# A spectral filter and a routed expert layer: the weights' maxima spread by TensorE, five experts loaded through SyncE, rank products moved

## The chip, the cores and the metric

The program runs on one core of a Trainium2 chip. Its engines are TensorE (PE, with its weight load PEld), VectorE (DVE), ScalarE (ACT), GpSimd (POOL) and SyncE (SP, which issues DMA transfers). The metric is the device time of one execution in microseconds, as the median of the runs shown; lower is better. Profiles are of one execution each.

## The reference

```
X = rfft(x, axis=1); y = irfft(X * (filt_r + 1j * filt_i), n=2496)      # x: 8 x 2496 x 256
x = y.reshape(19968, 256)
xn = x / (norm(x) + 1e-6); en = expert_emb / (norm(expert_emb) + 1e-6)  # 8 experts
logits = xn @ en.T / tau; expert_idx = argmax(logits)
probs = exp(logits - max); probs /= sum + 1e-9; gate = probs[expert_idx]
for e in range(8):                                                      # w1: 256 x 1024, w2: 1024 x 256
    out[mask] = gate * (relu(x[mask] @ w1[e]) @ w2[e])
```

Everything is fp32 at the outside. Each token goes to one expert.

## The kernel before

The 8 batches are 8 groups. A length of 2496 is 64 x 39, so the transform is a product over 39, one over 64, the filter, and the two inverse products. For a batch g these are `conv_s1` (tiles s), `conv_s2` (tiles s2, then the filter in yy and xs, then sa) and `conv_sb` (tiles y: the inverse over 39). The first batch has its own form, `conv_first`: its first product and its turned copies stay in SBUF, inside the array W in which the experts' weights will lie later (`turned`, `filter_first`). yy and xs are made by VectorE and added by POOL (L527, L621 for later batches).

`conv_sb` also routes. Of 8 token tiles (a chunk) `route` makes logits, the one-hot tile oh and, by products on TensorE (rk, "rank products", L812 to L815), each token's place in its expert's list. Then POOL scatters each row to DRAM (XS, L841), one scatter for a tile; `rows_out` casts the place to an integer on VectorE ahead of each (L834). A route is a generator with three steps; `part` takes one step of it and sends out one tile's scatter, twice in an iteration of `conv_sb`.

Then come slots. A slot is 256 rows of one expert: its rows come transposed from XS (xT), `up` makes ph and h (h in two f16 parts, ScalarE and VectorE), `down` makes po, and the output is scattered by POOL (L941). A slot has four steps fp. Group 0 has 8 slots, one an expert, and runs beside the stages of batch 1; so on for each group, and at last come blocks of 128 rows for what didn't fit.

An expert's weights are used as two f16 parts, high and low, scaled by a power of two. For that `weight_load` fetches w1 and w2 as fp32 (1 MB each) into the place of the next expert in W; `weight_halves` searches the largest magnitude: `largest` on VectorE within a partition (L258), `spread_max` over the partitions, which is an all-reduce on POOL (L262). Then `scales` makes the factors and `halves` the parts: ScalarE the high part (L284, L285, L289), POOL (L286) or VectorE (L290) the low one. `weight_halves` is a generator (`prep`): for each expert the search of the next one, then four quarters of its halves. The eighth expert's weights come last, in two parts.

What sets the order: while the first batch runs (`head`), the four engines but POOL keep the order of the program text (`manual_schedule`), and two tables of step numbers say at which steps a weight load (`WLOADS`) and a step of `prep` (`PREPS`) stand. After it a scheduler orders all engines by its own timeline; `spread`, called twice in each fp, takes a step of `prep`, and of the loads at each second call. A slot can't begin before its expert's halves are written (`prepped`). POOL is ordered by the scheduler throughout. Each engine runs its instructions strictly in its order.

Of the kernel before, what the change touches and what calls it, by code (L numbers as in the profile page):

```python
# [51 lines left out]
FAHEAD = 6  # L52
WLOADS = (4, 7, 11, 15, 21, 27)
PREPS = (15, 17, 23, 25, 27, 29, 31, 33, 41, 45, 49, 53, 57, 61)


@with_exitstack
def moe_spectral_kernel(
# [117 lines left out]
    def experts_ready():  # L176
# [10 lines left out]
        ehl = cw.tile([E, 2, D], F16, tag="hl", bufs=XYB, name="ehl")  # L187
        nc.scalar.copy(ehl[:, 0], esc)
        nc.vector.tensor_tensor(out=ehl[:, 1], in0=esc, in1=ehl[:, 0], op=ALU.subtract)
# [18 lines left out]
    wmax = const.tile([P, E, 2], F32, tag="wmax", name="wmax")  # L208
    wall = const.tile([P, E, 2], F32, tag="wall", name="wall")
    wsc = const.tile([P, E, 2], F32, tag="wsc", name="wsc")  # L210
# [30 lines left out]
    def weight_loads():  # L241

        for e in range(E - 1):
            for j in range(2):
                weight_load(nc.scalar, e, j)
                yield
# [3 lines left out]
    def weight_halves():  # L250
# [10 lines left out]
        def spread_max(e, js):  # L261
            nc.gpsimd.partition_all_reduce(wall[:, e, js], wmax[:, e, js], P, bass.bass_isa.ReduceOp.max)  # L262

        def scales(e, js):
            v.tensor_scalar(out=wall[:, e, js], in0=wall[:, e, js], scalar1=2.0 ** -100, scalar2=None, op0=ALU.max)
            v.tensor_scalar(out=wsc[:, e, js].bitcast(I32), in0=wall[:, e, js].bitcast(I32), scalar1=0x7F800000,
                            scalar2=0x7F800000, op0=ALU.bitwise_and, op1=ALU.bitwise_xor)
            for j in range(js.start, js.stop):
                v.tensor_scalar(out=wsc[:, e, j:j + 1], in0=wsc[:, e, j:j + 1], scalar1=2.0 ** (13 if j else 5),
                                scalar2=None, op0=ALU.mult)  # L270
            v.reciprocal(winv[:, e, js], wsc[:, e, js])
            if js.stop == 2:
                v.tensor_tensor(out=isc[:, e:e + 1], in0=winv[:, e, 0:1], in1=winv[:, e, 1:2], op=ALU.mult)
# [18 lines left out]
        def maxima(e):  # L292
            while (e, 1) not in raws:
                next(loads)
            for j in range(2):
                largest(e, j)
                if j:
                    spread_max(e, slice(0, 2))
                yield
# [12 lines left out]
        for j, order in ((0, (0, 1)), (1, (3, 2))):  # L312
            yield
            weight_load(nc.sync, e, j)
            yield
            yield
            largest(e, j)
            spread_max(e, slice(j, j + 1))
            yield
            scales(e, slice(j, j + 1))  # L320
            for k in order:
                halves(e, k)
                yield
# [133 lines left out]
    HALF = P * NK2  # L457
    turned = [big[:, n * 2 * HALF:(n + 1) * 2 * HALF].rearrange("p (h q) -> p h q", h=2) for n in range(2)]
    by_k2 = [t.rearrange("p h (q k) -> p h q k", k=NK2) for t in turned]

    def filter_first(k2):

        at = 4 * HALF + k2 * CW
        if at + CW <= big.shape[1]:
            ft = big[:, at:at + CW].rearrange("p (r c) -> p r c", r=2)
# [296 lines left out]
    def route(g, out_rows, t0, n, rows, ssq, rr, lp):  # L762
# [42 lines left out]
        yield 1  # L805

        base = state["base"]
        state["base"] = nbase = rt.tile([P, E], F32, tag="base", name=f"base{tg}")
# [284 lines left out]
    with tc.manual_schedule(engines=engines):  # L1093
        for n, _ in enumerate(head()):
            if n in WLOADS:
                next(loads, None)
            if n in PREPS:
                next(prep, None)
# [11 lines left out]
    def spread():  # L1110

        run["n"] = run.get("n", -1) + 1
        if run["n"] % 2 == 0:
            next(loads, None)
# [129 lines left out]
```

## Time and profile before

| what | value |
|---|---|
| median of 3 runs | 1433.49 us (1433.06 to 1438.99) |
| profiled execution, its own time | 1423.8 us |
| its span | 1422.0 us, mean granted clock of TensorE 0.94 |
| TensorE busy | 1260.9 us (89%) |
| VectorE, ScalarE, POOL busy | 872.5 (61%), 707.6 (50%), 562.9 us (40%) |
| DMA | 218.68 MB, mean 154 GB/s |

Busy time counts instructions that compute; an engine that waits or issues a transfer isn't busy. A row of waits names who waited, for which work, the sum, how often and the longest. In a timeline the bracket at the end of a row is the idle time before it and what ended it ("issue": nothing that the profile shows). The granted clock is a share of 2.4 GHz, so 0.50 is 1.2 GHz.

### The profile page before, as it was taken

The page shows a single profiled execution, that of the slowest core. Times are in us where ns is not written, and L with a number is a line of the kernel's source. Part 1 is how long each engine was busy: PE and PEld are TensorE (multiplying, and loading weights), DVE is VectorE, ACT ScalarE, POOL GpSimd, SP SyncE. Part 2 cuts the span into 40 slices and gives each one's busy share as a digit, 9 for nine tenths or more (in the row PEclk, how much of TensorE's full clock was granted, in tenths as well). Part 3 has the DMA queues.
Part 4 walks back from the last instruction along what each step waited for, and adds up shares of the span by engine and source line. Part 5 has one row for each costly group of instructions (what it writes and reads, how often), then busy time and mean ns, then how long its engine had stood idle before and what let it go on. Part 6 is the DMA issues. An engine that isn't in the chain of part 4 may idle for free.

```text
span 1422.0 us, 32280 instructions
## 1 busy us (share of the span) xinstructions
PE 1260.9 (89%) x11144; PEld 1000.3 (70%) x11144; DVE 872.5 (61%) x2842; ACT 707.6 (50%) x1600; POOL 562.9 (40%) x630
## 2 busy tenths in 40 slices
PE   6546275889699989999999999999999999999998
PEld 5333153557376876778687778777787888999997
DVE  2637457748447675867567576658567832366664
ACT  3456045646256465557646664755576333333333
POOL 1323412524542753464264527444631741222221
PEclk8868578899799999999999999999999999999999
DMA  8312395465777777676767666766764432122221
GB/s 292 125 45 79 94 307 187 149 163 158 210 205 191 194 222 188 167 210 196 207 161 217 200 173 186 225 193 165 200 185 120 112 95 52 43 53 50 47 44 42
DMA packets 221610, 218.68 MB, mean 154 GB/s; under 512 B 125197, under 2 KB 166125, under 8 KB 219520
## 3 DMA queue, kind: packets, MB, share of 16 engines
q1 hardware_dynamic: 192558, 141.44, 38.3%
q0 software_dynamic: 26592, 60.28, 13.7%
q10 hardware_dynamic: 2290, 14.81, 2.8%
q8 instruction: 93, 1.52, 0.5%
q14 instruction: 77, 0.63, 0.1%
HBM read 116.37 MB, written 79.60 MB: 138 GB/s over the span
## 4 chain that ended last, share of the span: by engine, by line
PE 41%; issue 11%; DMA 5%; POOL 4%; DVE 2%; ACT 2%; SPq 0%; POOLq 0%; DVEq 0%; ACTq 0%
PE ph L1006 15%; PE po L1034 14%; PE y L427 4%; POOL out_dram L941 3%; PE s L427 2%; PE sa L432 2%; PE s L432 2%; PE tp L736 2%; DMA a<-SD 1%; DMA f<-ZD 1%; DMA ZD<-z 1%; PE lp L751 1%; DMA XS<-rows,ixi 1%; DMA f<-in_filt 1%; DVE xs L587 1%
## 5 line engine op out<-in xcount | busy, mean ns | idle before, releaser
L1034 PE MATMUL po<-W,h 128*128 128x256 f16 (+1 forms) x3864 | 499.8, 274 | 1.2 <-ACT h L1012 1.0
L1006 PE MATMUL ph<-xT,W 128*128 128x256 f16 x3072 | 405.2, 277 | 47.3 <-DMA xT<-XS 24.5
L1034 PEld LDWEIGHTS <-h 128*128 128x128 f16 x3864 | 370.7, 98 | 88.0 <-issue 44.5
L1006 PEld LDWEIGHTS <-W 128*128 128x128 f16 x3072 | 298.6, 99 | 136.5 <-issue 92.0
L1012 ACT ACTIVATE h<-ph 128x512 f16<-128x512 f32 (+1 forms) x388 | 203.8, 526 | 302.1 <-PE ph L1006 233.6
L1013 DVE SCALAR_TENSOR_TENSOR h<-ph,h 128x512 f16<-128x512 f32 (+1 forms) x388 | 231.9, 598 | 189.5 <-ACT h L1012 187.7
L941 POOL DMA_INDIRECT out_dram<-o,meta x161 | 171.7, 1066 | 316.8 <-ACT o L1041 270.2
L841 POOL DMA_INDIRECT XS<-rows,ixi x176 | 174.6, 992 | 124.6 <-issue 71.7
L621 POOL TENSOR_TENSOR yy<-yy,xs 128x512 f32<-128x512 f32 x70 | 93.6, 1343 | 99.0 <-DVE xs L587 66.7
L387 POOL DMA_DIRECT2D in<-in_x x84 | 67.7, 807 | 145.4 <-PE s L427 114.7
L1006 PE MATMUL ph<-xT,wp 128*128 128x128 f16 x1584 | 104.8, 219 | 0.0
L1006 PEld LDWEIGHTS <-wp 128*128 128x128 f16 x1584 | 96.7, 98 | 2.6
L994 DVE COPY wp<-W 128x1024 f16 x132 | 61.3, 465 | 49.6 <-PE ph L1006 48.9
L717 ACT ACTIVATE rows<-y 128x256 f16<-128x256 f32 x176 | 66.2, 385 | 48.5 <-PE y L427 47.9
L692 DVE SCALAR_TENSOR_TENSOR rows<-y,rr,rows 128x256 f16<-128x256 f32 x176 | 77.1, 478 | 20.1 <-ACT rows L689 18.4
L427 PE MATMUL s<-in,c_sb 117*128 117x512 f32 (+1 forms) x168 | 87.7, 608 | 1.4 <-ACT z L642 1.2
L427 PE MATMUL y<-f,csb_sb 120*128 120x512 f32 (+1 forms) x168 | 83.1, 579 | 4.1 <-DMA f<-ZD 4.0
L689 ACT ACTIVATE rows<-y,rr 128x256 f16<-128x256 f32 x176 | 74.0, 475 | 24.9 <-DVE rr L722 23.3
L585 DVE TENSOR_TENSOR yy<-s,f 128x256 f32<-128x256 f32 x140 | 53.1, 419 | 51.1 <-ACT xs L614 45.0
L1041 ACT ACTIVATE o<-po,meta 128x256 f32<-128x256 f32 x161 | 69.5, 475 | 24.1 <-PE po L1034 23.3
L451 ACT COPY s<-s 128x512 f32<-128x512 f32 x77 | 45.3, 588 | 53.8 <-PE s L427 49.5
L587 DVE SCALAR_TENSOR_TENSOR xs<-xs,sgn_sb,f 128x256 f32<-128x256 f32 x140 | 68.6, 531 | 0.0
(196 smaller groups left out, 1502.3 us busy)
## 6 DMA issues: line engine op xcount, KB each, us to landing
f<-in_filt SPq DMA_DIRECT2D x148, 256.0 KB
a<-SD SPq DMA_DIRECT2D x70, 256.0 KB
ZD<-z SPq DMA_DIRECT2D x70, 256.0 KB
SD<-s SPq DMA_DIRECT2D x70, 240.0 KB
f<-ZD SPq DMA_DIRECT2D x70, 240.0 KB
in<-in_x POOLq DMA_DIRECT2D x70, 234.0 KB, 4.4
W<-in_w ACTq DMA_DIRECT2D x14, 1024.0 KB
W<-in_filt SPq DMA_DIRECT2D x12, 256.0 KB
```

The source lines that it names most:

```text
L427: nc.tensor.matmul(out_, c[:a.shape[0]], a, start=True, stop=True)
L587: nc.vector.scalar_tensor_tensor(out=o, in0=i, scalar=sgn_sb[:, k2:k2 + 1], in1=f, op0=ALU.mult, op1=ALU.mult)
L621: nc.gpsimd.tensor_tensor(out=yy, in0=yy, in1=xs, op=ALU.add)
L689: nc.scalar.activation(rows[:, i, 0:D], y[:, i], AF.Copy, scale=rr[:, u:u + 1])
L692: nc.vector.scalar_tensor_tensor(out=rows[:, i, D:2 * D], in0=y[:, i], scalar=rr[:, u:u + 1], in1=rows[:, i, 0:D], op0=ALU.mult, op1=ALU.s ...
L841: i = nc.gpsimd.indirect_dma_start(out=XS, out_offset=bass.IndirectOffsetOnAxis(ap=ix, axis=0), in_=src, in_offset=None)
L941: i = nc.gpsimd.indirect_dma_start(out=out, out_offset=bass.IndirectOffsetOnAxis(ap=idx, axis=0), in_=o, in_offset=None, bounds_check=NT - ...
L1006: last["pe"] = nc.tensor.matmul(ph[:, fi, :size], wp[:, k * 2 + wh, fi * P:(fi + 1) * P], xT[:, xh * 2 + k], start=(c == 0), stop=(c == 5))
L1012: last["relu"] = nc.scalar.activation(h[:, 0, :, :size], ph[:, :, :size], AF.Relu)
L1013: hd = nc.vector.scalar_tensor_tensor(out=h[:, 1, :, :size], in0=ph[:, :, :size], scalar=0.0, in1=h[:, 0, :, :size], op0=ALU.max, op1=ALU. ...
L1034: nc.tensor.matmul(self.po[:, s], self.hs[fp][:, hh, fi, s * P:(s + 1) * P], self.Wp[:, off + wh * 1024:off + wh * 1024 + D], start=(fp == ...
L1041: nc.scalar.activation(o, self.po[:, s], AF.Copy, scale=self.meta[:, s, 1:2])
```

## The change

Four things change. `spread_max` no longer uses POOL: the maxima are cut to a power of two, a product of TensorE with a unit matrix turns a column of 128 maxima into a row (pm), VectorE takes the row's maximum (wtop) and writes it on a small diagonal (wdg), and a second product with ones spreads it to all partitions (ps). These are two further steps of `prep` for each search. The loads of the head go through SyncE in place of ScalarE, and ten stand there in place of six, five experts; to make room `turned[1]` moves to the end of W. `PREPS` has 24 steps in place of 14, the last eight at the head's last step: four experts are searched and two split there, before three and two. And in the first batch the first two chunks' rank products wait three steps of `part` longer.

```diff
--- before.py
+++ after.py
@@ -50,8 +50,8 @@
 DLAG = 2
 MID = 8
 FAHEAD = 6
-WLOADS = (4, 7, 11, 15, 21, 27)
-PREPS = (15, 17, 23, 25, 27, 29, 31, 33, 41, 45, 49, 53, 57, 61)
+WLOADS = (0, 1, 8, 12, 30, 34, 38, 42, 46, 50)
+PREPS = (16, 20, 22, 24, 26, 30, 36, 38, 40, 42, 44, 46, 52, 56, 60, 62) + (90,) * 8
 
 
 @with_exitstack
@@ -185,7 +185,7 @@
         esc = cw.tile([E, D], F32, tag="hl", bufs=XYB, name="esc")
         nc.vector.tensor_scalar(out=esc, in0=emb_sb, scalar1=en1, scalar2=64.0, op0=ALU.mult, op1=ALU.mult)
         ehl = cw.tile([E, 2, D], F16, tag="hl", bufs=XYB, name="ehl")
-        nc.scalar.copy(ehl[:, 0], esc)
+        nc.vector.tensor_copy(ehl[:, 0], esc)
         nc.vector.tensor_tensor(out=ehl[:, 1], in0=esc, in1=ehl[:, 0], op=ALU.subtract)
         nc.vector.tensor_scalar(out=tau64, in0=tau_sb, scalar1=64.0, scalar2=None, op0=ALU.mult)
         yield
@@ -206,7 +206,10 @@
     isc = const.tile([P, E], F32, tag="isc", name="isc")
 
     wmax = const.tile([P, E, 2], F32, tag="wmax", name="wmax")
-    wall = const.tile([P, E, 2], F32, tag="wall", name="wall")
+    one32 = const.tile([2, P], F32, tag="one32", name="one32")
+    nc.vector.memset(one32, 1.0)
+    wtop = const.tile([2, E], F32, tag="wtop", name="wtop")
+    wdg = const.tile([2, E, 2], F32, tag="wdg", name="wdg")
     wsc = const.tile([P, E, 2], F32, tag="wsc", name="wsc")
     winv = const.tile([P, E, 2], F32, tag="winv", name="winv")
     wmx = const.tile([P, 4], F32, tag="wmx", name="wmx")
@@ -242,7 +245,7 @@
 
         for e in range(E - 1):
             for j in range(2):
-                weight_load(nc.scalar, e, j)
+                weight_load(nc.scalar if last else nc.sync, e, j)
                 yield
 
     prepped = [0]
@@ -259,12 +262,25 @@
             v.tensor_reduce(out=wmax[:, e, j:j + 1], in_=wmx[:, :len(pieces)], axis=AX.X, op=ALU.max)
 
         def spread_max(e, js):
-            nc.gpsimd.partition_all_reduce(wall[:, e, js], wmax[:, e, js], P, bass.bass_isa.ReduceOp.max)
+
+            n = js.stop - js.start
+            m = wmax[:, e, js]
+            v.tensor_scalar(out=m, in0=m, scalar1=2.0 ** -100, scalar2=None, op0=ALU.max)
+            v.tensor_scalar(out=m.bitcast(I32), in0=m.bitcast(I32), scalar1=0x7F800000, scalar2=None,
+                            op0=ALU.bitwise_and)
+            yield
+            pm = ps_c.tile([P, P], F32, tag="c", name=f"pm{e}_{js.start}")
+            nc.tensor.matmul(pm[:n], m, ident32, start=True, stop=True)
+            v.tensor_reduce(out=wtop[:n, e:e + 1], in_=pm[:n], axis=AX.X, op=ALU.max)
+            v.tensor_scalar(out=wdg[:n, e, :n], in0=ident32[:n, :n], scalar1=wtop[:n, e:e + 1], scalar2=None,
+                            op0=ALU.mult)
+            yield
+            pm = ps_c.tile([P, 2], F32, tag="c", name=f"ps{e}_{js.start}")
+            nc.tensor.matmul(pm[:, :n], one32[:n], wdg[:n, e, :n], start=True, stop=True)
+            v.tensor_scalar(out=wsc[:, e, js].bitcast(I32), in0=pm[:, :n].bitcast(I32), scalar1=0x7F800000,
+                            scalar2=None, op0=ALU.bitwise_xor)
 
         def scales(e, js):
-            v.tensor_scalar(out=wall[:, e, js], in0=wall[:, e, js], scalar1=2.0 ** -100, scalar2=None, op0=ALU.max)
-            v.tensor_scalar(out=wsc[:, e, js].bitcast(I32), in0=wall[:, e, js].bitcast(I32), scalar1=0x7F800000,
-                            scalar2=0x7F800000, op0=ALU.bitwise_and, op1=ALU.bitwise_xor)
             for j in range(js.start, js.stop):
                 v.tensor_scalar(out=wsc[:, e, j:j + 1], in0=wsc[:, e, j:j + 1], scalar1=2.0 ** (13 if j else 5),
                                 scalar2=None, op0=ALU.mult)
@@ -295,7 +311,7 @@
             for j in range(2):
                 largest(e, j)
                 if j:
-                    spread_max(e, slice(0, 2))
+                    yield from spread_max(e, slice(0, 2))
                 yield
 
         yield from maxima(0)
@@ -315,7 +331,7 @@
             yield
             yield
             largest(e, j)
-            spread_max(e, slice(j, j + 1))
+            yield from spread_max(e, slice(j, j + 1))
             yield
             scales(e, slice(j, j + 1))
             for k in order:
@@ -455,13 +471,14 @@
 
     big = W32[:, E // 2:].rearrange("p e c -> p (e c)")
     HALF = P * NK2
-    turned = [big[:, n * 2 * HALF:(n + 1) * 2 * HALF].rearrange("p (h q) -> p h q", h=2) for n in range(2)]
+    ends = (slice(0, 2 * HALF), slice(big.shape[1] - 2 * HALF, big.shape[1]))
+    turned = [big[:, e].rearrange("p (h q) -> p h q", h=2) for e in ends]
     by_k2 = [t.rearrange("p h (q k) -> p h q k", k=NK2) for t in turned]
 
     def filter_first(k2):
 
-        at = 4 * HALF + k2 * CW
-        if at + CW <= big.shape[1]:
+        at = 2 * HALF + k2 * CW
+        if at + CW <= ends[1].start:
             ft = big[:, at:at + CW].rearrange("p (r c) -> p r c", r=2)
         else:
             ft = cf.tile([P, 2, D], F32, tag="f", name=f"f0_{k2}")
@@ -804,6 +821,10 @@
         v.tensor_tensor(out=oh, in0=w8.unsqueeze(1).to_broadcast([P, nt, E]), in1=bc(mv), op=ALU.is_equal)
         yield 1
 
+        if g == 0 and t0 + n // 2 < NAG // 2:
+            yield 1
+            yield 1
+            yield 1
         base = state["base"]
         state["base"] = nbase = rt.tile([P, E], F32, tag="base", name=f"base{tg}")
         rk = ps_c.tile([P, 2, NTC, E], F32, tag="c", name=f"rk{tg}")
@@ -1094,7 +1115,7 @@
         for n, _ in enumerate(head()):
             if n in WLOADS:
                 next(loads, None)
-            if n in PREPS:
+            for _ in range(PREPS.count(n)):
                 next(prep, None)
     tc.no_sync_barrier()
     enqueue(0)
@@ -1110,7 +1131,7 @@
     def spread():
 
         run["n"] = run.get("n", -1) + 1
-        if run["n"] % 2 == 0:
+        if run["n"] % 4 == 0:
             next(loads, None)
         next(prep, None)
         if run.get("table"):
```

In the order of POOL, at the middle of the first batch's second product (yy are the filtered tiles). Before:

```order
L527 TENSOR_TENSOR yy_3_418<-yy_3_418,xs_3_415 128x512
L262 ISA
L262 ISA wall<-wmax 128x2
L527 ISA
L527 TENSOR_TENSOR yy_4_450<-yy_4_450,xs_4_447 128x512
```

And now:

```order
L544 TENSOR_TENSOR yy_3_421<-yy_3_421,xs_3_418 128x512
L544 TENSOR_TENSOR yy_4_449<-yy_4_449,xs_4_446 128x512
L544 TENSOR_TENSOR yy_5_482<-yy_5_482,xs_5_479 128x512
L544 TENSOR_TENSOR yy_6_514<-yy_6_514,xs_6_511 128x512
L403 DMA in_0_669<-in_x 117x2x256
```

The all-reduce and the two configurations around it are gone; the adds follow each other.

In the order of VectorE, at the end of the head (ixi are row numbers of the scatters, adm and drop belong to the admission of rows, h to the first slot). Before:

```order
L829 RECIPROCAL rows_10_1130<-se_8_1332 128x2
L834 CAST ixi_4_1248<-ix_4_1246 128x1 x2
L834 CAST ixi_8_1361<-ix_8_1359 128x1 x6
L859 TENSOR_TENSOR adm_1395<-base_8_1346,ecap 128x8
L866 SCALAR_TENSOR_TENSOR adb_1401<-ecap,base_8_1346 128x8
L265 TENSOR_SCALAR wall<-wall 128x2
L861 SCALAR_TENSOR_TENSOR bad_1397<-thr,adm_1395 128x16
L266 TENSOR_SCALAR wsc<-wall 128x2
```

And now:

```order
L850 RECIPROCAL rows_10_1135<-se_8_1340 128x2
L855 CAST ixi_4_1289<-ix_4_1287 128x1 x5
L855 CAST ixi_8_1369<-ix_8_1367 128x1 x6
L285 TENSOR_SCALAR wsc<-wsc 128x1 x2
L287 RECIPROCAL winv<-wsc 128x2
L289 TENSOR_TENSOR isc<-winv 128x1
L306 SCALAR_TENSOR_TENSOR W<-W,wsc 128x1024 x3
L261 TENSOR_REDUCE wmx<-W 128x1 x2
L262 TENSOR_REDUCE wmax<-wmx 128x1
L261 TENSOR_REDUCE wmx<-W 128x1 x2
L262 TENSOR_REDUCE wmax<-wmx 128x1
L268 TENSOR_SCALAR wmax<-wmax 128x2
```

Five casts of the second chunk are left there in place of two, and behind them stand the second expert's scales and differences, the fourth's search and its spread.

In the order of SyncE, from the last filters of the first batch on (f are filters, SD the store of batch 1's first product). Before:

```order
L468 DMA f_18_513<-in_filt 128x512
L468 DMA f_19_515<-in_filt 128x512
L453 DMA SD_176<-s_0_676 120x2x256
L453 DMA SD_176<-s_1_717 120x2x256
L453 DMA SD_176<-s_2_790 120x2x256
```

And now:

```order
L485 DMA f_18_520<-in_filt 128x512
L485 DMA f_19_522<-in_filt 128x512
L228 DMA W<-in_w 128x2048 x2
L469 DMA SD_179<-s_0_677 120x2x256
L228 DMA W<-in_w 128x2048
L469 DMA SD_179<-s_1_726 120x2x256
L228 DMA W<-in_w 128x2048
L469 DMA SD_179<-s_2_800 120x2x256
```

Six of the ten loads stand here, one or two between the stores; the other four stand ahead of the filters f, between the first ones.

## Rows read from the trace of the kernel before

**Rows 1.** The page, busy time, share of the span and instructions of TensorE

```profile
PE 1260.9 (89%) x11144; PEld 1000.3 (70%) x11144; DVE 872.5 (61%) x2842; ACT 707.6 (50%) x1600; POOL 562.9 (40%) x630
```

**Rows 2.** Waits of TensorE, 0 to 440 us: total, times, longest (us)

```profile
PE sa L537 <- POOL yy L527: 33.6, 6, 16.6
PE ph L1006 <- DMA xT<-XS: 24.5, 3, 15.2
PE rk L812 <- DVE oh L804: 15.7, 3, 7.5
PE s L496 <- ACT W L498: 7.2, 1, 7.2
...
PE ph L1006 <- DVE wsc L269: 6.8, 2, 5.4
...
PE ph L1006 <- DVE wmax L259: 4.8, 1, 4.8
```

**Rows 3.** Stretches: busy us of PE, PEld, DVE, ACT, POOL; granted clock, DMA share, GB/s

```profile
4.00:26.00 22.00, 14.63 (x92) 13.88 (x92) 4.30 (x31) 6.10 (x13) 1.82 (x9) 0.82 0.99 333
26.00:92.00 66.00, 31.25 (x142) 22.98 (x141) 30.05 (x61) 29.39 (x46) 19.60 (x19) 0.71 0.33 115
92.00:163.00 71.00, 45.42 (x293) 26.26 (x294) 50.77 (x205) 34.42 (x98) 23.90 (x32) 0.74 0.29 81
...
178.00:252.00 74.00, 51.19 (x308) 35.19 (x308) 48.86 (x91) 33.41 (x48) 17.07 (x15) 0.81 0.80 245
252.00:299.00 47.00, 36.15 (x225) 25.00 (x223) 29.69 (x54) 27.77 (x40) 20.85 (x19) 0.88 0.41 127
299.00:365.00 66.00, 60.26 (x527) 42.89 (x525) 46.06 (x208) 35.75 (x102) 28.94 (x40) 0.97 0.60 167
365.00:386.00 21.00, 10.47 (x12) 3.30 (x13) 9.37 (x29) 5.81 (x10) 14.43 (x14) 0.56 0.83 248
386.00:514.00 128.00, 123.37 (x1005) 91.86 (x1005) 78.92 (x288) 69.75 (x167) 58.59 (x66) 1.00 0.74 199
```

**Rows 4.** Line 262, the all-reduce: duration min, median, max (ns); who waited

```profile
L262 POOLq MODIFY_POOL_CONFIG  x16: 1/37/62, 43.1 to 308.7; - x16
L262 POOL PARTITION_ALL_REDUCE wall<-wmax x9: 354/371/1226, 50.9 to 315.2; - x9
...
  DVE wall L265: 21.2, 5
```

**Rows 5.** Timeline of POOL around the first all-reduce: start, duration, work, idle before

```profile
41.83 1.27 POOL L527 TENSOR_TENSOR yy<-yy,xs 128x512 f32<-128x512 f32 x1 [2.72 <-DVE xs L478]
50.91 0.37 POOL L262 PARTITION_ALL_REDUCE wall<-wmax  x1 [7.81 <-issue]
58.27 3.71 POOL L527 TENSOR_TENSOR yy<-yy,xs 128x512 f32<-128x512 f32 x3 [6.99 <-issue]
```

**Rows 6.** Timeline of ScalarE, first stage

```profile
21.21 0.56 ACT L498 COPY W<-s 128x480 f32<-128x480 f32 x1 [6.08 <-DMA W<-in_filt]
```

**Rows 7.** DMA issues: operation, count, KB each

```profile
W<-in_w ACTq DMA_DIRECT2D x14, 1024.0 KB
```

**Rows 8.** Groups of VectorE, 0 to 400 us: count, busy us, mean ns

```profile
L258 DVE TENSOR_REDUCE wmx<-W 128x1 f32<-128x1024 f32 x31 | 36.4, 1212 | 3.6 <-DMA W<-in_w 3.6
...
L290 DVE SCALAR_TENSOR_TENSOR W<-W,wsc 128x1024 f16<-128x1024 f32 x23 | 30.9, 1359 | 19.1 <-ACT W L289 19.1
...
L1013 DVE SCALAR_TENSOR_TENSOR h<-ph,h 128x512 f16<-128x512 f32 x36 | 24.6, 686 | 29.6 <-ACT h L1012 29.4
...
L587 DVE SCALAR_TENSOR_TENSOR xs<-xs,sgn_sb,f 128x256 f32<-128x256 f32 x32 | 20.7, 685 | 0.0
...
L585 DVE TENSOR_TENSOR yy<-s,f 128x256 f32<-128x256 f32 x32 | 12.2, 418 | 24.6 <-ACT xs L614 20.8 <-DMA f<-in_filt 3.8
```

**Rows 9.** Timeline of POOL, the first batch's last scatter but one

```profile
171.22 0.99 POOL L841 DMA_INDIRECT XS<-rows,ixi  x1 [0.30 <-issue]
```

**Rows 10.** Timeline of TensorE, the first slot's first products

```profile
177.94 4.80 PE L1006 MATMUL ph<-xT,W 128*128 128x256 f16 x24 [15.17 <-DMA xT<-XS]
```

## The prediction

> **What bounds the kernel now.** I read the page first: TensorE is busy 89% of the span [rows 1], so what can be won is its idle time and the time it runs at the lower clock. The waits of TensorE say where that is: before 440 us the list is long, led by POOL (33.6 us), by transposed rows from DRAM (24.5) and by the one-hot tile of the routing (15.7) [rows 2]. The table of stretches says the same from the other side: from 386 to 514 us, a whole steady group, TensorE is busy 123.4 of 128 us at clock 1.00; from 178 to 386 us, where the first group does the same work, it has 208 us at 0.56 to 0.97, and before 178 us it is busy about half the time [rows 3]. So all that this change can win lies ahead of 386 us, and what comes behind, 1036 us, should stay.
>
> Why POOL is late is seen on POOL itself. Each of the nine all-reduces is bracketed by reconfigurations, 16 in all, 1 to 62 ns long in the trace [rows 4]; but the engine stands idle around them. At the first one it ends an add at 43.1, is idle 7.8 us, reduces for 0.4, is idle 7.0 and starts the next add at 58.3 [rows 5]: 15.2 us for a result of 128x2 numbers. The adds yy queued behind it are what TensorE waits for, 16.6 us at the longest [rows 2]; VectorE waits another 21.2 us for the results themselves [rows 4].
>
> **The change part by part.** I go through the span in stretches.
>
> *4 to 26 us.* ScalarE stands 6.1 us before a PSUM copy of the first stage, put down to a filter transfer [rows 6]; the instruction ahead of that copy in its program is a weight load, which waits for an earlier transfer. TensorE loses 7.2 us to it [rows 2]. The loads go to SyncE, so this wait goes: +7 us (bounds 4 and 7.2). SyncE now has four weight loads of 1 MB [rows 7] between the filters of the first stages. In bytes: 2.5 MB of x, 5.2 MB of filters and 4.2 MB of weights, 12 MB, at the 333 GB/s of this stretch [rows 3] are 36 us, so the last filter could land at 40 us; the last k-step should want it at about 46. I cost the transfers at nothing; without that slack each load would hold a filter 1.05 MB / 333 GB/s = 3.1 us, 12.6 us for four.
>
> *26 to 92 us.* TensorE is busy 31 of 66 us, VectorE 30 [rows 3]. The two all-reduces in it go: of the 33.6 us of waiting for yy [rows 2], six waits, I take 31, since the small ones belong to the lag of the loop and not to POOL's idle time (bounds 28 and 33.6). What takes their place on TensorE and VectorE: two tiny fp32 products, and three more small VectorE operations an expert, for which no row stands; the nearest above is a 0.7 us row of 128x256 numbers [rows 8], so at most 3 us an expert, beside VectorE's 36 idle us. Together the two stretches give 38: the inverse stage starts at 54 instead of 92.
>
> *92 to 163 us, the inverse stage.* VectorE is busy 50.8 of 71 us [rows 3], in chains of dependent small operations, and I take it as the limit here. The rank products stand three steps later on TensorE, so its 15.7 us of waiting for the one-hot tile [rows 2] can go, but only what VectorE itself idled for comes back. Against it stands more VectorE work: two reductions move into this stretch with a scaled difference, about 2 x 1.2 + 1.4 less one 1.4 [rows 8], 2.5 us. Net +3 (bounds -3 and +10).
>
> *163 to 178 us, the tail.* Before, two and six casts of row numbers stand behind the last chunk's ranks, and each frees one scatter; the last but one begins at 171.2, after 0.30 us of idle time, and takes 0.99 [rows 9], so they go out 1.29 us apart and the last ends by 173.5. The first product of the first slot starts at 177.9 [rows 10], 4.4 us later. In the new order five and six casts stand there, since the ranks of the second chunk come three steps later: 3 x 1.29 = -4. Behind them come an expert's halves, another's search and its spread, with two products on TensorE ahead of the first slot: five passes of ScalarE at about the 1.2 us of a VectorE pass [rows 8], 6, the last difference 1.4, four reductions 4.8 and some 3.5 for casts, scales and the spread are 15.7 us, while scatters and landing take 11 x 1.29 + 4.4 = 18.6. So they are just covered; were they not, it would cost up to 5. The first slot starts at 178 - 38 - 3 + 4 = 141.
>
> *178 to 365 us, the first group.* TensorE's waits here are for transposed rows, for wsc (6.8 us) and wmax (4.8) [rows 2], and VectorE's for the all-reduce [rows 4]; the clock is low behind each. In the new VectorE order slots 0 to 2 hold 12 reductions, 9 scaled differences, 12 second parts of h, and four steps of yy and xs: 12 x 1.21 + 9 x 1.36 + 12 x 0.69 + 8 x (0.42 + 0.69) = 43.9 us [rows 8], 47 with the small ones. TensorE needs less: a steady slot with its full share of the next batch's stages is 128 / 8 = 16 us [rows 3], 48 for three, and only five stage steps of a full share of some 16 stand here. So this part is VectorE's: 47 us in place of 74 (178 to 252), +27, of which I take 24 for the one wait for transposed rows that may stay, as 2 MB of loads are still issued there. From 252 to 299 two slots with their share are 32 us of the steady group; I take 35 for 47, +12. From 299 to 365 TensorE is busy 60.3 of 66 [rows 3]: +2. Bounds for the group: it can't go under the 128 us of the steady one [rows 3], +59; and if VectorE's waits for POOL become waits for TensorE's products, only the 21.2 us of [rows 4] less their new round trips are won, +10.
>
> *365 to 386 us, the seam to the second group.* TensorE's order still puts the last ranks behind all products of the first group, so the gap stays. Two output scatters move behind the last six row scatters: +2 (bounds 0 and 3).
>
> **A rule of the skill.** The first idle time is measured: 7.8 us ahead of a reduction and 7.0 behind it [rows 5]. The Trainium skill, GPSIMD Engine Reference, section Instruction dispatch, says that the first call of a freshly loaded kernel pays a code load of about 6 us (5.95 measured) that the profile shows no instruction for. The trace agrees that such a pause exists, but here it stands on both sides of each reduction and is longer. By the page's figure a reduction would hold POOL for 2 x 5.95 + 0.4 = 12.3 us, an estimate, and the two of the second stretch 25 in place of 30, so that the sum would be 5 smaller, 1361; the rows decide.
>
> **The sum.** 38 + 3 - 4 + 24 + 12 + 2 + 2 = 77 us. The profiled execution took 1423.8 us with a span of 1422.0; it would take 1347. The median of the runs is 9.7 us above the profiled one, so I forecast 1433.5 - 77 = 1356 us.
>
> **Rivals.**
> *A, as summed*, 60 to 98 us won, 1335 to 1373 us: 0.55.
> *B, the first group stays slow.* Its stalls have several owners in turn (transposed rows, VectorE, ScalarE's copies), and at 48.9 of 74 us [rows 3] VectorE is no idle engine. Then only the head's 37 and about 10 are won, and down to 38 if the tail isn't covered: 1373 to 1395 us, middle 1386: 0.24. Against it speaks that 21.2 us of VectorE's own waits are POOL's.
> *C, all waits of the head and the first group go.* 44 + 55 = 99 us and more, 1334 and below: 0.12. Against it: the seam and the VectorE sum.
> *D, slower: the two products of each spread stall TensorE.* They stand in its strict order, each behind a chain on VectorE, which itself has reductions queued. The dearest such waits in the list are 5.4 us for wsc and 4.8 for wmax. Nine searches with two products at 5.4 are 97 us, which is 20 over the gain: 1453 us. It decides from 77 / 18 = 4.3 us a product on. For it: wsc and wmax are there already; against: those very waits are, for wsc, the all-reduce's. 0.04. Here the Trainium skill, GPSIMD Engine Reference, section When to use GPSIMD, speaks against the change: it lists the cross-partition reduce as GpSimd's alone. No row shows one on TensorE yet.
> *E, the change doesn't do what it says:* the seam, which is paced by scatters, takes up what the first group wins, and the head's gain is eaten by filters behind weights (12.6) and stores of the next batch behind five more loads (15.7). Of 77 are left 77 - 40 - 12.6 - 15.7 = 9: 1425, at the edge of no change: 0.05.
>
> **How the numbers follow.** 1356 is A's. The range 1330 to 1393 holds A, nearly all of B and the upper third of C, and leaves out about 0.18; A's own range is 1335 to 1373. A measurement of this kernel can tell about 0.5% (7 us) from no change. Faster by more than that: A, B and C and a little of E, 0.92; within: 0.04; slower: 0.04.
>
> **What would show it.** No reconfiguration on POOL and no idle time of 7 us between its adds; the wait of TensorE for yy in the first stages under 4 us; the inverse stage starts at 54 us and the first slot at 141; slots 0 to 2 in about 47 us with VectorE busy over 85%; the seam still 19 us; from the second group on 1036 us as before. I would be wrong if the waits for wmax or for the spread's tiles exceed 2 us each, if the first slot starts after 150, or if the first group still needs over 165 us.

## The result, and the profile after

| | before | after |
|---|---|---|
| median | 1433.88 us (1433.06 to 1438.99, 4 runs) | 1388.16 us (1380.90 to 1391.90, 4 runs) |
| ratio, 95% interval | | 0.9668 (0.9621 to 0.9714) |
| profiled execution, its span | 1423.8, 1422.0 | 1380.9, 1379.0 |

45.7 us were won of 77 forecast. In a later set of runs the ratio was 0.9665 (0.9621 to 0.9710). The profiled execution of the new kernel is the fastest of its four, and that of the kernel before is faster than all four of its runs; the two spans differ by 43.0 us. Four of the runs below (the spread in spaced steps, loads through ScalarE, later loads, both) belong to a set in which every kernel, that of before too, took some 8% longer, in these four traces from about 410 us on, so that their times are read only as ratios to the kernel before in that set. The following table puts the same places of both traces beside each other; h is VectorE's second part of a slot's first hidden tile.

| place, us | before | after | won up to here |
|---|---|---|---|
| second stage starts on TensorE (first t) | 26.74 | 18.01 | 8.7 |
| inverse stage starts (first v) | 92.18 | 60.41 | 31.8 |
| last ranks of the first batch | 160.26 | 126.65 | 33.6 |
| first slot's first product | 177.94 | 148.75 | 29.2 |
| slot 0's first h | 181.32 | 152.14 | 29.2 |
| slot 3's first h | 251.94 | 208.36 | 43.6 |
| slot 5's first h | 299.26 | 246.45 | 52.8 |
| last h of the first group | 355.42 | 319.52 | 35.9 |
| first product of the second group | 386.19 | 340.08 | 46.1 |
| end | 1422.0 | 1379.0 | 43.0 |

The gain reaches 52.8 us at slot 5, and 17 of it are gone at the end of the last slot. The waits of TensorE up to 440 us (who waited, for whom: total, times, longest):

```profile
PE pm L273 <- DVE wmax L269: 15.7, 2, 13.2
PE ph L1027 <- DMA xT<-XS: 14.5, 2, 10.0
PE sa L656 <- POOL yy L638: 8.9, 1, 8.9
PE y L443 <- DVE q L737: 7.2, 2, 4.1
PE sa L554 <- POOL yy L544: 7.0, 5, 2.3
PE rk L833 <- DVE ixi L855: 5.9, 1, 5.9
PE ph L1027 <- POOL W L302: 5.2, 1, 5.2
```

Of [rows 2], the 33.6 us for the head's yy are 7.0, those for the one-hot tile and for ScalarE's copy in the first stage are gone, and three belong to the first group and its seam: slot 1's rows (10.0 us), expert 7's weights (5.2) and yy in the seam (8.9). Of these only the second is new. In the trace of before slot 1's rows and the seam's yy were waited for as well:

```profile
197.65 2.74 PE L1006 MATMUL ph<-xT,W 128*128 128x256 f16 x12 [7.85 <-DMA xT<-XS]
380.08 2.07 PE L639 MATMUL sa<-yy,m_sb 128*128 128x512 f32 x2 [5.35 <-POOL yy L621]
```

The stretches of the head, and of the first group from slot 0's first h on (length, busy us of PE, PEld, DVE, ACT, POOL; granted clock, DMA share, GB/s):

```profile
18.00:60.40 42.40, 32.19 (x144) 23.34 (x144) 28.62 (x59) 23.99 (x40) 15.90 (x16) 0.80 0.71 255
60.40:126.60 66.20, 43.39 (x291) 25.01 (x292) 47.38 (x187) 33.91 (x96) 19.26 (x27) 0.78 0.45 142
126.60:148.70 22.10, 3.69 (x15) 1.89 (x16) 15.26 (x52) 5.86 (x6) 14.47 (x14) 0.50 0.33 88
...
152.14:208.36 56.22, 43.56 (x317) 32.95 (x316) 42.76 (x74) 31.83 (x47) 15.85 (x12) 0.88 0.87 204
208.36:246.45 38.09, 35.18 (x221) 23.13 (x221) 20.75 (x51) 21.58 (x36) 18.88 (x18) 0.96 0.60 178
246.45:305.35 58.90, 49.27 (x395) 33.45 (x396) 48.34 (x180) 36.71 (x97) 24.05 (x33) 0.92 0.65 185
305.35:319.50 14.15, 12.08 (x92) 8.09 (x91) 10.18 (x48) 5.00 (x9) 4.89 (x5) 0.74 0.23 63
319.50:343.00 23.50, 13.26 (x71) 7.70 (x70) 8.38 (x33) 6.66 (x12) 14.96 (x15) 0.78 0.85 242
```

TensorE is idle 12.7 us in slots 0 to 2, 9.6 in slots 5 and 6 and 10.2 in the seam. Rows from the timelines of SP's queue and of TensorE show the first: slot 1's transposed rows are issued at 151.23, and the product that needs them starts at 170.33. Those of slot 0, issued at 145.44, were there at 148.75.

```profile
145.44 1.34 SPq L996 DMA_TRANSPOSE xT<-XS  x1
...
151.23 1.26 SPq L996 DMA_TRANSPOSE xT<-XS  x1
```

```profile
170.33 2.72 PE L1027 MATMUL ph<-xT,W 128*128 128x256 f16 x12 [10.00 <-DMA xT<-XS]
...
300.28 4.45 PE L1027 MATMUL ph<-xT,W 128*128 128x256 f16 x20 [5.20 <-POOL W L302]
...
336.52 2.07 PE L656 MATMUL sa<-yy,m_sb 128*128 128x512 f32 x2 [8.90 <-POOL yy L638]
```

The owner of the other two is POOL, in order of time: expert 7's low half (L302) stands behind eight row scatters that go out 1.29 us apart, and the adds yy behind fourteen more and two output scatters.

```profile
286.68 1.09 POOL L862 DMA_INDIRECT XS<-rows,ixi  x1 [7.37 <-DVE ixi L855]
...
298.07 2.16 POOL L302 TENSOR_TENSOR W<-W 128x1024 f16<-128x1024 f32 x1
...
331.65 0.89 POOL L862 DMA_INDIRECT XS<-rows,ixi  x1 [0.30 <-issue]
332.85 1.01 POOL L962 DMA_INDIRECT out_dram<-o,meta  x1 [0.30 <-issue]
334.17 1.00 POOL L962 DMA_INDIRECT out_dram<-o,meta  x1 [0.30 <-issue]
335.17 3.73 POOL L638 TENSOR_TENSOR yy<-yy,xs 128x512 f32<-128x512 f32 x3
```

### The profile page after: what moved, and what is told of

It is laid out like the page before. It is cut to its first block, busy times and chain, and to the rows that moved or that the text cites. A ratio compares the mean times of both kernels' runs of the same rounds, so it can differ in the third digit from the quotient of the medians.

```text
span 1379.0 us, 32360 instructions
## 1 busy us (share of the span) xinstructions
PE 1257.2 (91%) x11180; PEld 998.9 (72%) x11180; DVE 875.8 (64%) x2871; ACT 705.4 (51%) x1599; POOL 560.8 (41%) x621
## 3 DMA queue, kind: packets, MB, share of 16 engines
q1 hardware_dynamic: 193998, 151.93, 42.4%
q0 software_dynamic: 26592, 60.28, 14.4%
## 4 chain that ended last, share of the span: by engine, by line
PE 54%; issue 12%; DMA 5%; POOL 5%; DVE 1%; ACT 1%; SPq 0%; POOLq 0%; ACTq 0%; DVEq 0%
PE ph L1027 19%; PE po L1055 18%; PE y L443 4%; PE s L443 4%; POOL out_dram L962 3%; PE sa L448 3%; PE tp L753 2%; DMA a<-SD 2%; PE s L448 2%; DMA f<-ZD 2%; PE lp L768 1%; PE sa L656 1%; DMA ZD<-z 1%; POOL XS L862 0%; POOL yy L638 0%
## 5 line engine op out<-in xcount | busy, mean ns | idle before, releaser
L734 ACT ACTIVATE rows<-y 128x256 f16<-128x256 f32 x176 | 66.2, 385 | 49.5 <-PE y L443 49.0
L1062 ACT ACTIVATE o<-po,meta 128x256 f32<-128x256 f32 x161 | 69.5, 476 | 21.6 <-PE po L1055 17.4
L753 PEld LDWEIGHTS <-rows 128*128 128x128 f16 x704 | 48.9, 99 | 27.3 <-issue 23.5
```

Source lines behind the costliest of these rows:

```text
L753: nc.tensor.transpose(tp[:, i, j], rows[:, i, j * P:(j + 1) * P], ident)
L1062: nc.scalar.activation(o, self.po[:, s], AF.Copy, scale=self.meta[:, s, 1:2])
```

## The experiments

Ratios are to the kernel before in the same set of runs. Two smaller edits of the change are taken back by no run of their own: the copy of ehl from ScalarE to VectorE, and the loads behind the head, one at every fourth call of `spread()` in place of every second.

**The spread alone, in one step** (`e1_spread_alone`). In the kernel before:

```diff
-            nc.gpsimd.partition_all_reduce(wall[:, e, js], wmax[:, e, js], P, bass.bass_isa.ReduceOp.max)
+            (the changed kernel's spread_max, without its two yields;
+             what scales did to the maxima ahead of the factors goes)
```

> The kernel before with nothing changed but the way of a maximum to all partitions (TensorE instead of the all-reduce on POOL), each in one step of the preparation. Theory P (POOL's idle time around each all-reduce is most of the head's gain): the waits of TensorE for yy before 92 us fall from 33.6 us to under 8, the inverse stage starts at 60 to 66 instead of 92 us, and the time is 1390 to 1405 us. Rival L (the loads through SyncE and the new order are needed for it; a spread right behind its search stalls TensorE instead): under 20 us won, 1415 us and more, with waits for wmax of over 3 us each.

Measured: 1437.9 us, ratio 0.9962 (0.9927 to 0.9998); the inverse stage starts at 87.75. POOL's part went as theory P says: yy took 33.6 us of waiting, and takes 4.5. But TensorE's timeline has the first products of the two spreads of the second stage, each after a wait:

```profile
45.65 0.59 PE L272 MATMUL pm<-ident,wmax 128*2 128x128 f32 x2 [7.00 <-DVE wmax L269]
67.51 0.59 PE L272 MATMUL pm<-ident,wmax 128*2 128x128 f32 x2 [7.62 <-DVE wmax L269]
```

In TensorE's strict order they stand right behind their search, which VectorE ends 7 us after TensorE has come to them. Rival L's numbers come out. What was won at the inverse stage, 4.4 us, doesn't reach the slots: the first slot starts at 177.52, before at 177.94, and in the first group slot 2 waits 16.3 us, put down to a weight load, where the kernel before has no such wait. So the 5 us are what is left of the spread in this order, not its price on TensorE alone.

**The spread alone, in steps of its own** (`e5_spread_spaced`). As above, with the two yields and 20 steps of `PREPS` in place of 14, so that the same searches and halves stay in the head.

> The kernel before with the spread on TensorE, now with the search, the first product and the second product in steps of their own, with other products between them; the number of experts prepared in the head, the loads and all the rest as before. Theory G (the spread alone won so little, 0.996 of before, because each product stood right behind its search in TensorE's strict order and waited 7.0 and 7.6 us there): the waits for wmax ahead of 92 us fall from 14.6 us to under 6, the inverse stage starts at 68 to 78 us, the time is 15 to 25 us below before, 1411 to 1421. Rival L (the loads through ScalarE bring the weights too late, so that any place near there waits): the inverse stage still starts after 82 us and the time is within 8 us of before.

Measured: 0.9921 (0.9890 to 0.9953); the inverse stage starts at 78.75, and the waits for wmax ahead of it are two:

```profile
43.57 0.59 PE L273 MATMUL pm<-ident,wmax 128*2 128x128 f32 x2 [4.70 <-DVE wmax L269]
61.94 0.59 PE L273 MATMUL pm<-ident,wmax 128*2 128x128 f32 x2 [6.68 <-DVE wmax L269]
```

Between the theories: the first product stands two head steps behind its search and waits 4.7, then one step and waits 6.7. In the changed kernel they are two steps, 2.46 us, and six, no wait:

```profile
37.78 0.58 PE L273 MATMUL pm<-ident,wmax 128*2 128x128 f32 x2 [2.46 <-DVE wmax L269]
```

The wait gets shorter with the gap, as theory G has it, though the same two steps cost 4.7 us in one kernel and 2.46 in the other. Late weights are not the reason: up to 64 us VectorE stands idle ahead of no reduction of a search. It won 12 us and not 15, and 11.4 us of waits were left where G had 6.

**The all-reduce back in the changed kernel** (`e2_allreduce_back`).

```diff
         def spread_max(e, js):
-            (all but its two yields)
             yield
+            nc.gpsimd.partition_all_reduce(wall[:, e, js], wmax[:, e, js], P, bass.bass_isa.ReduceOp.max)
             yield
 (and scales cuts the maxima to a power of two again)
```

> The changed kernel with the all-reduce on POOL again, all steps of the preparation where the change put them. Theory P: five searches in the head bring five pauses of some 15 us on POOL, of which the adds yy behind them hand most to TensorE; the time is 1420 to 1450 us, so that the rest of the change is worth little or less than nothing without the spread. Rival L (loads and order carry the gain): 1405 us or below.

Measured: 0.9851 (0.9803 to 0.9900). Between the two: loads, places and order are worth 21 us without the spread, and the spread 26 more on top (0.9851 less 0.9668), against 5 alone. POOL's idle time is back, 5.6 to 8.7 us ahead of each reduction, and the adds yy hand it on in the head and in the group. Of POOL's timeline the reductions with the shortest and the longest idle time, then waits of TensorE up to 440 us:

```profile
42.83 0.55 POOL L267 PARTITION_ALL_REDUCE wall<-wmax  x1 [5.59 <-DVE xs L485]
...
275.74 0.38 POOL L267 PARTITION_ALL_REDUCE wall<-wmax  x1 [8.70 <-DMA xT<-XS]
```

```profile
PE sa L646 <- POOL yy L628: 31.4, 5, 12.1
PE ph L1017 <- DMA xT<-XS: 23.6, 2, 21.2
PE sa L544 <- POOL yy L534: 19.3, 5, 15.0
```

**The head's loads through ScalarE** (`e6_loads_scalar`).

```diff
-                weight_load(nc.scalar if last else nc.sync, e, j)
+                weight_load(nc.scalar, e, j)
```

> The changed kernel with the ten weight loads of the head through ScalarE's queue again, at the same steps. By the forecast's term (+7, bounds 4 and 7.2): the first stage's wait for ScalarE comes back with 4 to 8 us, the inverse stage starts that much later, and the time is 4 to 10 us above the changed kernel (0.967 of before). Rival: two queues take the loads and the filters side by side, so the last filter lands sooner and what the first stage loses comes back at the end of the k loop: within 3 us of it.

Measured: 0.9774 (0.9736 to 0.9813); the inverse stage starts at 68.63, the first slot at 160.99, where the run with later loads in the same set has 59.38 and 151.67. The first t is at 26.98, the changed kernel's at 18.01: the loss of some 9 us stands in the first stage, as the forecast's +7 has it, though the record now names x's own tiles (four waits, 9.4 us) and not ScalarE. The copy of ehl stays on VectorE here, so it isn't what won this stage. The time missed its expectation: 0.0106 above the change's 0.9668 are 15 us of before's time, not 4 to 10. Some 9 of them are the first stage; from the first slot's product to the second group's first h this run takes 207.3 us, the change 194.3 and (in a second profile) 196.9, and what holds it there is open.

**Ranks and tail** (`e3_ranks_back`, `e8_ranks_alone_back`, `e9_tail_free`). The first was meant to take back the ranks' place alone:

```diff
-        if g == 0 and t0 + n // 2 < NAG // 2:
-            yield 1
-            yield 1
-            yield 1
```

> The changed kernel without the three extra steps ahead of the rank products of the first batch's first two chunks. By the forecast's terms (+3 in the inverse stage, -4 in the tail): TensorE's waits for the one-hot tile come back with some 10 us in three or more waits, the inverse stage is 3 us longer, the tail 4 us shorter, the time within 5 us of 1388. Rival (the move is what makes the inverse stage as short as it is): 8 us or more slower.

It has six steps less in the head, so step 90, with the last eight of `PREPS`, never came, and it took back two things; its time, 11 us below the changed kernel, is where neither side had put it. The next two part them: ranks back with `(84,) * 8`, and the changed kernel without `(90,) * 8`.

> The earlier run with the ranks back had six steps less in the head, so that the eight steps of preparation of the last step (expert 3's search and spread, expert 2's halves) fell out of the tail too and came in the slots. Here the ranks are back and these eight stay in the tail. Theory T (the eight steps in the tail are what costs): within 5 us of the changed kernel. Theory K (the ranks' new place is what costs): 8 to 14 us faster than the changed kernel.

> The changed kernel with its new place of the ranks, but without the eight steps of preparation in the tail; they come in the slots, one for each call. Theory T: 8 to 14 us faster than the changed kernel, since TensorE's order then has the last ranks of the second batch some 60 products ahead of the second group's first one instead of 13, and the 14 scatters behind them are hidden; the seam (last ranks to the second group) is no gap any more. Theory K: no faster.

| ranks | eight steps in the tail | ratio (95%) | inverse stage, us | tail to the first slot, us |
|---|---|---|---|---|
| moved | yes (the change) | 0.9668 (0.9621 to 0.9714), 0.9665 (0.9621 to 0.9710) | 66.2, 69.8 | 22.1, 22.3 |
| back | yes | 0.9706 (0.9665 to 0.9747) | 68.7 | 23.7 |
| moved | no | 0.9667 (0.9624 to 0.9710) | 66.3 | 21.6 |
| back | no | 0.9574 (0.9537 to 0.9612) | 69.0 | 17.9 |

The second values of the first line are from the changed kernel run again (`after_again`):

> The changed kernel once more, beside the next three on one chip: 0.967 of before.

The inverse stage doesn't follow the ranks' place. With the ranks back, TensorE waits 9.9 us for ixi and 5.0 or 5.4 for the one-hot tile, in place of 5.9 for ixi alone, and the stage is as long. The tail does follow: taking back both brings 4.2 us, the eight steps alone 0.5, the ranks alone nothing. Neither T nor K is right as stated: either undone alone wins nothing, both undone are 0.9% faster than the change. In the tail the scatters and the eight steps run beside each other, so either of the two alone keeps it at 22 to 24 us, and only without both is it 17.9. Of the some 13 us the tail shows 4. In the second group, from the h of its slot 1 to that of the third group's slot 1, the run with both back takes 137.9 us, the change 140.5 and 144.3 in its two profiles, the kernel before 136.8; that is 2.6 to 6.4 more. What does it there is open, and the last line's run was made in another set than the two above it.

**Denser preparation** (`e4_prep_denser`). One more step of `prep` at every fourth call of `spread()`:

```diff
         if run["n"] % 4 == 0:
             next(loads, None)
+            next(prep, None)
```

> The changed kernel with five steps of the weights' preparation for every four calls behind the head instead of four. Theory S (each spread adds two steps to the preparation, so that the last expert's halves come six steps later than before, behind eight row scatters on POOL, and slot 7 waits for them): the 5.2 us wait of TensorE for W<-POOL near 295 us is gone, slots 5 and 6 take under 50 us instead of 59, the time is 6 to 15 us below 1388. Rival V (VectorE, busy 45 of 50 us there, is the limit, and the wait only shows where): the time stays within 4 us of 1388, and the wait moves to h or yT.

Measured: 0.9635 (0.9599 to 0.9671), not to be told from the change. The wait for expert 7's half went, and from the first slot's first product the last h comes after 156.0 us in place of 170.8. But the second group's first product comes after 191.9, where it was 191.3: the seam took all of it. TensorE waits there for yy behind 22 row scatters in a row (with two output scatters among them), the first at 305.66, the last at 336.07:

```profile
338.32 2.07 PE L656 MATMUL sa<-yy,m_sb 128*128 128x512 f32 x2 [8.02 <-POOL yy L638]
```

Theory S had the right wait and the wrong price; V's number came out, though VectorE isn't what holds the seam: it is busy 16.6 of 38 us there.

**Later loads** (`e10_loads_later`).

```diff
-        if run["n"] % 4 == 0:
+        if run["n"] > 7 and run["n"] % 2 == 0:
```

> The changed kernel with the four weight loads behind the head at calls 8, 10, 12 and 14 instead of 0, 4, 8 and 12, so that no weights move while slot 1's rows do. Theory X (those rows, issued at 151.2 and landed at 170, stand behind 1.8 MB of filters and chunks on their own queue and beside 2 MB of weights): the 10.0 us wait of slot 1 falls under 4, 5 to 8 us faster than the changed kernel (0.961 to 0.963 of before). Rival Q (what is ahead of them in their own queue decides): the wait stays over 8 us and the time within 3 us. Rival W (the later weights hold the search of expert 5): a wait for wmax or wsc of over 3 us in slots 2 and 3, and no gain.

Measured: 0.9624 (0.9589 to 0.9659), where X had put it, but not to be told from the change's 0.9668. Theory X holds for the wait: slot 1's rows, issued at 154.21, are there when the product is due at 164.14, with no idle time. Slots 0 to 2 take 48.0 us (155.05 to 203.04). The issue of the rows, and the stretch around these slots:

```profile
154.21 1.25 SPq L996 DMA_TRANSPOSE xT<-XS  x1
```

```profile
152.00:204.00 52.00, 46.85 (x335) 35.25 (x333) 45.80 (x77) 32.95 (x48) 18.79 (x12) 0.92 0.77 238
```

From the first slot's first product, slot 5 has its h 8 us ahead of both profiles of the change (89.3 us in place of 97.7 and 97.2), the last h comes no more than 4.4 ahead, and the second group's slot 1 has its h after 209.9 us in place of 205.6 and 208.2. So the 8 us are given back, the last of them in the seam, where TensorE again waits 8.7 us for yy.

**The next batch's stages earlier** (`e7_steps_sooner`).

```diff
-            run["pace"] = steps / (4 * len(queue) - MARGIN)
+            run["pace"] = steps / (4 * len(queue) - (9 if g == 1 else MARGIN))
```

> The changed kernel with the next batch's stages paced for 23 calls instead of 29 in the first group alone. Theory T (the seam is 14 row scatters of 1.29 us behind the last ranks, at most 18 us, of which 10 us are idle time of TensorE): the last ranks stand 55 products ahead of the second group and the idle time of the seam falls under 4 us; 6 to 12 us faster than the changed kernel. Rival V (VectorE carries the stages and the preparation and gets later by what the seam wins): within 4 us of it.

Measured: 0.9590 (0.9550 to 0.9630), 1376.33 us beside 1389.17 for the changed kernel in the same set. Beside the second profile of the change, of that set, the last ranks come at 307.08 instead of 328.38, the last scatter at 321.91 instead of 337.10 (331.65 in the first profile), and the seam's wait is gone; slot 7 waits longer for expert 7:

```profile
315.31 4.45 PE L1027 MATMUL ph<-xT,W 128*128 128x256 f16 x20 [7.83 <-POOL W L302]
...
331.88 1.12 PE L656 MATMUL sa<-yy,m_sb 128*128 128x512 f32 x2 [0.46 <-POOL yy L638]
```

Theory T holds for the seam and for the time; for the time the traces show another place than the seam. From the first slot to the h of the second group's slot 1 it takes 204.8 us, the change 205.6 and 208.2. From there to the third group's slot 1 it takes 135.5 us, the change 140.5 and 144.3, the kernel before 136.8.

**Both** (`e11_both`), the edits of the last two together.

> The later loads of the run above together with the earlier stages of the next batch (23 calls) in the first group. Theories X and T together: 0.959 less 0.004 to 0.006, thus 0.953 to 0.955 of before, and the seam without idle time of over 4 us. Rival Q: 0.959.

Measured: 0.9629 (0.9593 to 0.9665), beside 0.9624 for the later loads alone. No gain adds up: slot 1's wait and the seam's are both gone, slot 7's first h is at 319.29, and the second group's slot 1 at 354.85 (354.58 without the later loads). What binds then is expert 7's preparation, with 6.9 us of waiting for its low halves. The denser preparation together with the earlier stages would try that; it wasn't run.

## Why the prediction was right and wrong

The sign, the place (all ahead of the second group) and the range held; the time fell into rival B's stretch, 1373 to 1395, not into A's, whose own range, 1335 to 1373, ends 15 us below it. By the terms of the sum:

| term | forecast | measured | what stood there |
|---|---|---|---|
| 4 to 26 us | +7 | +8.7 | shown by the loads through ScalarE: some 9 |
| 26 to 92 us | +31 | +23.0 | yy still waits 7.0, a spread 2.5 |
| inverse stage | +3 | +1.8 | 66.2 us, again 69.8 in a second profile |
| tail | -4 | -4.4 | |
| slots 0 to 2 | +24 | +14.4 | slot 1's rows, 10.0 us in place of 3 |
| slots 3 and 4 | +12 | +9.2 | |
| slot 5 to the last h | +2, for 299 to 365 us | -16.9 | expert 7 and the next batch's stages |
| seam | +2 | +10.2 | 20.6 us in place of 30.8 |
| second group on | 0 | -3.1 | 1038.9 us in place of 1035.8, 1043.9 in a second profile |

But for rounding the measured column sums to 43.0, with the seam taken from the last h to the second group's first product. It comes from one profile of each kernel. The second profile of the change is 10.5 us longer: 3.6 of it in the inverse stage, 3.0 from slot 5 to the last h, 5.0 from the second group on. So the small terms, the inverse stage's above all, can't be told from this scatter; the others are larger than it.

*The head.* The mechanism was right: no all-reduce is left, and the longest wait for yy went from 16.6 to 2.3. I mis-sized it by counting 31 of 33.6 us as POOL's pauses. TensorE has 32.2 us of work in the 42.4, at a clock of 0.80, and of the 10.2 that it is still idle 7.0 are five small waits for yy, which have no all-reduce behind them, and 2.5 a spread's first product. And I took the spread as the whole cause; the runs say that it is worth 5 us without the spaced steps and the loads, and 26 with them. Rival D's mechanism, which I held at 0.04, is thus real at 7 us a product when the products stand right behind their search. The change escapes it by the distance, and in the tail because the scatters take longer than the wait. The Trainium skill, GPSIMD Engine Reference, section When to use GPSIMD, gives the cross-partition reduce to GpSimd alone; the trace differs. In the first experiment, where nothing stands between, the spread took 1.9 us from the first product's start at 45.65 to the second's end at 47.51; POOL's took 15.2 from one add's end to the next one's start [rows 5].

*Inverse stage and tail.* Both terms came out, that of the inverse stage within its scatter (66.2 and 69.8 us). That TensorE isn't the limit there is shown by the ranks: 9 us of its waits come and go with their place, and the stage is 66 to 70 us either way. That VectorE is, busy 47.4 of 66.2 us, fits but isn't shown. "Just covered" was right for the eight steps: TensorE waits 13.2 us for a maximum, under the scatters, and leaving them out brings 0.5.

```profile
142.37 0.58 PE L273 MATMUL pm<-ident,wmax 128*2 128x128 f32 x2 [13.21 <-DVE wmax L269]
```

*The first group, where the step failed.* From its first product to its last h it still needs 170.8 us (before 177.5), and I had named 165 as the mark of an error; the mark on waits for wmax, 2 us, was passed too, with 2.5 and 13.2. Two sentences failed. The first is "of which I take 24 for the one wait for transposed rows that may stay": 3 us allowed, 10.0 measured, and the trace of before already had 7.85 at this place. With no weights on the way (the later loads) the wait is gone and slots 0 to 2 take 48.0 us, beside the 47 forecast, so VectorE's sum was right (it is busy 88% there, 76% in the change) and the transfer was the mis-sized term. The second is worse: from 299 us on I took the 91% for which TensorE was busy as a floor that nothing could raise, and gave it +2. It lost 17. Two causes are seen in the trace: each spread adds two steps to `prep`, so that expert 7's first half comes six steps later, behind eight scatters on POOL; and slot 7 stands further back in TensorE's order, with 395 products from slot 5's first h to slot 7's in place of the 330 of before:

```profile
299.26:343.01 43.75, 40.81 (x330) 28.10 (x329) 31.31 (x128) 27.01 (x80) 15.42 (x23) 0.97 0.65 175
```

Both hang on the late preparation: with the denser one the wait is gone, 324 products stand there, and the last h comes 14.8 us sooner, nearly all of the 17. It won nothing by it, since the seam grew by as much, to 35.9 us. So the seam's +10.2 in the table is the other side of the -16.9, and luck where the forecast had +2.

*Where the gain went.* What ends the first group is a chain in POOL's queue: the last ranks, 14 row scatters, yy, TensorE. Three edits took away one wait each, and by the second group's slot 1 most or all had come back at another place of that chain: slot 1's rows (8 us ahead at slot 5, gone behind the seam), expert 7 (15 us ahead at the last h, gone behind the seam), the seam (9 us gone, 2.6 more at slot 7, and 0.8 to 3.4 ahead). The third still won 13 us of time. The largest part of it that the traces show lies in the second group, and that is where the change itself loses 3.7 to 7.5 us against the kernel before (140.5 and 144.3 in place of 136.8), a term that the forecast put at nothing. Why the second group runs longer behind a late seam, these runs don't show. A seam that takes up what the slots win is rival E's mechanism, here at a part of its price. Rival B's reason, several owners in turn, is the better description; I had it at 0.24, against 0.55 for A.

## What to carry to other kernels

A wait in a list is worth its length only if nothing behind it on the same chain is late by as much; sum the stretch up to the next place where engines meet, and ask which queue sets that place, before the waits ahead of it are counted as gain. When an operation moves to an engine with a strict order, its price depends on the distance between its producer and its place in that order: here 7.0 and 7.6 us for the same product at no step, 6.7 at one, 4.7 and 2.5 at two, and none at six, with what else the producer's engine has to do in between. A step that is inserted in a shared generator makes everything later in that generator late, too: count the steps to the last consumer, not only the new instructions.

## What was unexpected of the hardware

A transposed load of one slot's rows took 3.3 us behind a stretch with a DMA share of 0.33, and 19 (151.23 to 170.33) with 1.8 MB of filters and chunks ahead of it and 2 MB of weights beside it; without those weights it was there within 9.9 (154.21 to 164.14). And POOL's idle time returned with every all-reduce at any place of the program, 5.6 to 8.7 us ahead of each of the nine in the run that put them back, not only at the first.
